# A fused attention, Fourier mixing and FFN kernel: batch 2's updates, group 1's preparation, the last W2 sums and the last stores are moved

## The chip, the cores and the metric

The kernel runs on one core of one Trainium2 chip. The time is the device time of one execution in microseconds (us). The kernel before was timed in three runs (median 777.29 us), and one more execution was recorded by the hardware profiler.

The engines are named as in the profile: PE (TensorE matmuls), PEld (its weight loads), DVE (VectorE), ACT (ScalarE), POOL (GpSimd), SP (the engine that issues DMAs here). A name with a q behind it (SPq) is that engine's queue. Each engine works through its own instructions in a fixed order.

## The reference

```
x = sink_window_attention(q, k, v)     # 4 batches, 8 heads, 768 tokens, 64 per head; 4 sink tokens, window 128
X = real(fft(fft(x, axis=tokens), axis=512 features))
u = x + X
un = (u - mean(u)) / sqrt(var(u) + 1e-6)          # over the 512 features
out = u + max(un @ w_ch1, 0) @ w_ch2              # w_ch1: 512 x 2048, w_ch2: 2048 x 512
```

All of it is float32. A matmul in full precision is made here from a high and a low part of each operand ("hi" and "lo", type fp32r): hi*hi + hi*lo + lo*hi. So most tensors are followed by a cast on ACT (hi) and a subtraction on DVE or POOL (lo).

## The kernel before

**Attention and Fourier transform.** The attention runs as a software pipeline of 96 steps (4 per block of 128 tokens, 24 blocks), with the steps that follow for what is still in the pipe. Into each step events are hung: `at(s, engine, fn)` makes `fn` be issued in step s on one engine's turn. The turns of a step come in the order S (loads), A (ACT), four numbered ones, V (DVE), G (POOL), T (PE). When the fourth block of a batch is stored, `fourier` hangs that batch's events behind that step: step 73 for batch 2 (the third batch), step 97 for batch 3 (the last). They are:
- folds of the first half of the tokens onto the second (`fold_n`, L347, then `fold_m`, L354 and L357) for j = 0, 1, 2, beginning at offsets 0, 4 and 8, with the hi cast on ACT (`fold_hi`, L360, tile gh) and the lo part on DVE (`fold_lo`, L363, tile gl). For the last batch all folds are on DVE (`FOLD_TAIL` = "VV")
- the middle row: `mid_sum` (L367) and `mid_row` (L371 the hi copy into sph, L373 its lo part), both on DVE
- stage 1 on PE (za, zr, zb, L390), casts of these to SBUF (L397, L405), stage 2 on PE (dc and a, L417; b, L438), copies of dc and a on ACT (`dc_copy`, L421, into the one-buffered tile dcs; `a_copy`, L426)
- `combine` (L443, L444): a - b and a + b into a tile d of three buffers
- `update` (L452 to L455): d is added to two blocks of u, one with the features in order and one reversed, two instructions each. For batches 2 and 3 the first is on DVE and the second on POOL (`UPD_TAIL` = "VG"). Batches 0 and 2 stay in SBUF; those of 1 and 3 are stored to DRAM.

An update of batch 2 is hung at offset `max(UPD_LATE + n, k) + 1`, n = 0 to 5, where k is the offset at which its combine is reached; with UPD_LATE = 24 k is always the larger.

**The order.** Up to step 97 (`CUT`) the order on each engine is that of the program. From there to the end of the first FFN group the order is made by the language's planner, which takes the program's order as a priority and its own modelled times for the rest. The FFN of groups 1 to 5 is again in the program's order.

**Weights.** The weights arrive as 64-bit values and are brought into shape by `convert(i)`, i = 0 to 31 (2f for w_ch1's slice f, 2f + 1 for w_ch2's): three instructions on DVE (L596 to L598), a hi cast on ACT (L620), the lo part on POOL (L621). For the first two w_ch2 slices the converted value itself is not kept; after the attention POOL adds hi and lo again into w2r (L1110), from which the W2 sums are made later.

**FFN, group 0.** The 24 blocks of tokens make six groups of four. Group 0 runs over 16 slices f of the hidden layer: `ch1` (12 matmuls of 512 columns, L632), relu on ACT and its lo part on DVE (L1121, L1126), `ch2` of the slice before (12 matmuls, L1133). In each f two steps of the remaining events are issued (`PER_F` = 2), so that steps 110, 111 fall on f = 0, and so on, and two weights are converted. At f = `PREP` = 11 the tiles of the relu are exchanged for others (h_sums; the tile un_last also begins here), and `prepare(1)` begins: statistics and normalisation of group 1's four blocks (L510 to L534), four turns on PE (L540), and hi (L544) and lo (L549) of the turned blocks into un_last. It is a generator of 20 pieces, and four are taken in each f from PREP on.

**FFN, groups 1 to 5.** Here w_ch2's product is made by a scheme of Strassen's kind: pairs q = 0 to 7 of hidden slices, seven products per pair (`product`, L1307), each of two halves (tp) of three matmuls of 256 columns. Its left operands are sums of the hidden layer (`first_h`, `second_h`, `third_h`: L1255 to L1268, tile h_sums). Its right operands, sums of W2, are made once, during group 1, stored to DRAM (w2s), and read again for each pair of the later groups in five loads by SP (`load_w2`, L1288) into one set of tiles WC (shown as w_ring and w2t). As there is one set, a load can only be issued when the products of the pair before have read the tile. The products of a pair run interleaved with `ch1` of the next pair.

**The end.** After the last pair `finish_last` makes its seven products and adds the seven accumulators p1 to p7 into the four quarters of the output, x11, x12, x21, x22 (each 128 partitions by two blocks by 256 features; L1329 is the helper `add`, L1382 the copy of p1 to s1, L1391 the sum s2 = s1 + p7). Four stores on SP, one per block of 128 x 512, follow when all quarters of two blocks are complete (L1399). Behind that, each engine reads a flag and branches (L1485, L1486) over a general version of the kernel that these inputs don't need.

Of the kernel before, what the change touches and what calls it, by code (L numbers as in the profile page):

```python
# [11 lines left out]
F32 = mybir.dt.float32  # L12
# [7 lines left out]
P = 128  # L20
# [24 lines left out]
Q_KEYS = (0, 1, 2, 4, 5, 6)  # L45
PTB = 3
W_FOLD = 6
NWA, PER_F, PREP = 14, 2, 11
FOLD_TAIL, UPD_TAIL = "VV", "VG"
UPD_LATE = 24  # L50
DSB, LDB = 3, 3
CONV_AT, CH1_AT = (3, 5, 7, 9), (9, 10)
CUT, MAN0 = 97, False
# [157 lines left out]
def kernel(  # L211
# [54 lines left out]
    def run(general):  # L266
        tag = "g" if general else ""
        with ExitStack() as p1:
# [59 lines left out]
            def fourier(b, at, ready):  # L328
# [36 lines left out]
                def mid_sum():  # L365
                    r = t_["x0"]
                    V.tensor_tensor(r[:, 1:256], r[:, 1:256], r[:, 511:256:-1], op=ALU.add)  # L367

                def mid_row():
                    t = t_["x0"]  # L370
                    V.tensor_copy(sph[:NR, :257], t[:, :257])  # L371
                    lo = sph[NR - 1:NR, :257]
                    V.tensor_tensor(lo, t[NR - 1:NR, :257], f32(lo), op=ALU.subtract)  # L373

# [95 lines left out]
                    at(k + F_S[1], "V", lambda j=j: fold_lo(j))  # L470
                at(ready[0] + ROW[0], "V", put_row)
                at(ready[0] + ROW[1], "V", mid_sum)
                at(ready[0] + ROW[2], "V", mid_row)
                k = ready[2] + S1
                n1, na, nb = PARTS_TAIL if tail else PARTS[b]
# [110 lines left out]
            def convert(i, pool=None):  # L586
# [14 lines left out]
                if i < 4:  # L601

                    if i == 0:
                        state["ring"] = npool.tile([P, 8, 512], F32R, tag="ring", name="w_ring", bufs=1)
                    d = [state["ring"][:, 2 * i + j] for j in range(2)]
                    if which:
                        state["w2t", f] = state["ring"][:, 2 * i:2 * i + 2]
                elif which:

                    if f == 2:  # L610
                        state["w2t", f] = pool.tile([P, 2, 512], F32R, name="w2t2")
                    d = [state["w2t", f % 3][:, j] for j in range(2)]
                elif W_FOLD <= f < W_FOLD + NHALF:

                    if f == W_FOLD:
                        state["fold"] = [npool.tile([P, NHALF, DM], F32R, tag=t, name=f"w_{t}", bufs=1) for t in ("gh", "gl")]
                    d = [t[:, f - W_FOLD] for t in state["fold"]]
                else:
                    d = [pool.tile([P, 512], F32R, name=f"w{i}_{j}") for j in range(2)]
                A.copy(d[0], tf)  # L620
                G.tensor_tensor(d[1], tf, f32(d[0]), op=ALU.subtract)  # L621
                Wt[f, which] = d
# [484 lines left out]
            ps_o = p1.enter_context(tc.tile_pool(name="ps_o" + tag, bufs=1, space=PSUM, side="right"))  # L1107
            wa = p1.enter_context(tc.tile_pool(name="wa" + tag, bufs=1, side="right"))
            for f in range(2):
                G.tensor_tensor(w2_raw(f, wa).bitcast(F32), *(f32(x) for x in Wt[f, 1]), op=ALU.add)  # L1110
            pg = ExitStack()
            g0 = pg.enter_context(tc.tile_pool(name="g0" + tag, bufs=1, side="right"))
            def relu(g, f, ps):
# [168 lines left out]
                V.tensor_tensor(t2, b22, t1, op=ALU.subtract)  # L1282
                V.tensor_tensor(t4, b21, t2, op=ALU.subtract)

            def load_w2(q, i):

                c, k, n, at_ = PARTS_W[i]
                nc.sync.dma_start(f32(WC[c][:, :, 2 * P * k:2 * P * (k + n)]), w_dram[q][:, :, 2 * P * at_:2 * P * (at_ + n)])  # L1288
# [9 lines left out]
                V.tensor_tensor(lo, src, f32(hi), op=ALU.subtract)  # L1298
                nc.sync.dma_start(w_dram[q][:, :, 2 * P * at_:2 * P * (at_ + n)], f32(t))

            def product(acc, q, i, tp):

                a, (c, k) = i, RIGHT[i]
                hi, lo = (t[:, 2 * P * a + P * tp:2 * P * a + P * tp + P] for t in (hc_hi, hc_lo))
# [69 lines left out]
            def finish_last(g, acc, q):  # L1374

                (x11, x12), (x21, x22) = halves(g)
                p1, p7, p2, p4, p5, p6, p3 = (bank2(t) for t in acc)
                s1, s2 = wl.tile([P, 2, 2 * P], F32, tag="u2", name=f"u2_{g}", bufs=1), r4[:, 0]
                for i in range(4):
                    for tp in range(2):  # L1380
                        product(acc, q, i, tp)
                A.copy(s1, p1)  # L1382
                add(G, x11, s1)
                add(V, x21, p4)
                add(V, x11, p2)
                for i in (5, 4, 6):
                    for tp in range(2):
                        product(acc, q, i, tp)
                add(V, s1, p6)
                add(G, x12, s1)  # L1390
                V.tensor_tensor(s2, s1, p7, op=ALU.add)  # L1391
                add(G, x21, s2)
                add(V, x22, p5)
                add(V, x22, s2)
                add(V, x12, p5)
                add(V, x12, p3)
                for t in (1, 0):
                    for b, blk in groups[g][2 * t:2 * t + 2]:
                        nc.sync.dma_start(out[b, blk], u_of(b, blk))  # L1399

            prev, late, turns = None, iter(()), []
            with tc.manual_schedule():
                w_sums(0)
# [2 lines left out]
                for g in range(1, len(groups)):  # L1406
                    unT = state[g][1]
                    steps = iter(())
                    for q in range(NF // 2):
# [12 lines left out]
                        if prev is not None:  # L1422
# [4 lines left out]
                                finish_a(*prev[:2])  # L1427
                            if g == 1:
                                w_sums(q)
                            else:  # L1430
                                load_w2(q, 1)
                                load_w2(q, 0)
                        if q == 1 and g == 1:
                            finish(0, po, us, slice(1, 4))
                        elif q == 1:
                            finish_c(*old)
                            late = finish_d(old[0])
# [6 lines left out]
                        slot(prev, slice(7, 14))  # L1444
                        second_h()
                        if g > 1:
                            for i in range(2, 5):
                                load_w2(q, i)
                        elif q:
                            for i in (1, 0, 2):  # L1450
                                split_w(q, i)
# [113 lines left out]
```

## Time and profile before

| | |
|---|---|
| runs | 777.29 us (median of 3; 776.57 to 779.79) |
| the profiled execution | 777.47 us, span of its instructions 775.7 us |
| PE busy | 741.1 us (96% of the span) |
| DVE busy | 601.3 us (78%) |
| ACT busy | 344.1 us (44%) |
| POOL busy | 186.4 us (24%) |
| mean granted clock of PE | 0.993 |

The attention and the Fourier transform fill the span until about 240 us, group 0 of the FFN ends about 337 us, and groups 1 to 5 take the rest. In a row of the timeline stand start, length (us), engine, line, operation, output and inputs, shapes and count; in brackets the engine's idle time ahead of it and what ended that. In the chain of waits each row is a piece of work (start, length, engine, tile, line), and the pieces together lead to the last instruction. In the windows the columns behind the length are busy us (and instructions) of PE, PEld, DVE, ACT and POOL, the granted clock, the busy share of the DMA engines and GB/s.

### The profile page before, as it was taken

To read this page: it belongs to the slowest core of one execution; us is meant where nothing else is said; L and a number is where in the kernel's file an instruction comes from. 1 tells how busy PE (TensorE), PEld (TensorE's weight loads), DVE (VectorE), ACT (ScalarE), POOL (GpSimd) and SP (SyncE) were. 2 spreads that over 40 slices of the span, in tenths; PEclk is the share of its full clock that TensorE was granted. 3 is DMA by queue.
4 is the path that set the end of the run, shared out by engine and by line. 5 is a ranking of instruction groups with operands and counts; after the bars stand their busy time and mean duration, and the time that the engine had idled before them with its cause. 6 is when DMAs were issued, how large, how long until landed. Compare 5 with 4: busy or idle time off the path is not lost.

```text
span 775.7 us, 14193 instructions
## 1 busy us (share of the span) xinstructions
PE 741.1 (96%) x4915; PEld 626.8 (81%) x4915; DVE 601.3 (78%) x1640; ACT 344.1 (44%) x893; POOL 186.4 (24%) x288
## 2 busy tenths in 40 slices
PE   7999998998989999999999999999999999999993
PEld 5666776766777878778888989989999989998992
DVE  6778589789799989959877978778895788664344
ACT  5777666666633323344545333333343334432330
POOL 2557368377555445300000000000000000000002
PEclk9999999999999999999999999999999999999997
DMA  9845515533304456224446766655666557555653
GB/s 292 266 125 155 142 55 166 142 110 113 110 28 122 151 190 217 92 100 165 161 168 227 231 188 214 229 184 170 210 213 216 171 177 232 165 188 176 220 175 113
DMA packets 96224, 131.23 MB, mean 169 GB/s; under 512 B 5996, under 2 KB 61420, under 8 KB 95760
## 3 DMA queue, kind: packets, MB, share of 16 engines
q1 hardware_dynamic: 95856, 126.49, 51.2%
q0 software_dynamic: 288, 3.76, 1.2%
q8 instruction: 41, 0.67, 0.4%
q14 instruction: 39, 0.32, 0.1%
HBM read 106.09 MB, written 24.13 MB: 168 GB/s over the span
## 4 chain that ended last, share of the span: by engine, by line
PE 80%; DVE 13%; ACT 2%; issue 2%; DMA 1%; POOL 1%; SPq 0%; ACTq 0%; DVEq 0%; POOLq 0%
PE h L632 32%; PE p L1307 25%; PE o L1133 4%; PE xt L802 4%; PE s L715 4%; PE za L390 2%; PE pt L764 2%; PE zb L390 1%; DVE f L347 1%; DVE sm L733 1%; PE zr L390 1%; DVE s L721 1%; PE x L814 1%; DVE gl L363 1%; DMA vt<-in_v_sink_dram 1%
## 5 line engine op out<-in xcount | busy, mean ns | idle before, releaser
L1307 PE MATMUL p<-w_ring,h_sums 128*128 128x256 f32 x960 | 134.5, 283 | 1.9 <-DMA w_ring<-w2s 1.7
L1307 PEld LDWEIGHTS p<-w_ring,h_sums 128*128 128x128 f32 x960 | 126.0, 191 | 5.4 <-issue 1.9
L1255 ACT CAST h_sums<-sums 128x256 fp32r<-128x256 f32 (+2 forms) x160 | 90.8, 567 | 70.9 <-PE p L1307 31.3
L1307 PE MATMUL p<-w2t,h_sums 128*128 128x256 f32 x720 | 112.9, 283 | 0.0
L1256 DVE TENSOR_TENSOR h_sums<-sums,h_sums 128x256 fp32r<-128x256 f32 (+2 forms) x160 | 99.5, 622 | 15.1 <-ACT h_sums L1255 14.0
L1329 POOL TENSOR_TENSOR u<-u,u 128x512 f32<-128x512 f32 x2 | 2.8, 1376 | 434.9 <-ACT u L1382 431.3
L1307 PEld LDWEIGHTS p<-w2t,h_sums 128*128 128x128 f32 x720 | 100.3, 191 | 3.1
L632 PE MATMUL h<-un_last,w 128*128 128x512 f32 x396 | 96.5, 392 | 0.0
L632 PE MATMUL h<-un_slots,w 128*128 128x512 f32 x396 | 96.3, 391 | 0.0
L632 PEld LDWEIGHTS h<-un_slots,w 128*128 128x128 f32 x396 | 72.7, 188 | 14.1
L632 PEld LDWEIGHTS h<-un_last,w 128*128 128x128 f32 x396 | 72.2, 188 | 14.5 <-DVE un_slots L549 0.7
L739 ACT ACTIVATE sm<-sm,mx 128x132 f32<-128x132 f32 x192 | 75.9, 400 | 14.4 <-DVE mx L733 14.4
L1441 ACT ACTIVATE sums<-h 128x512 f32<-128x512 f32 x40 | 23.9, 598 | 98.3 <-PE h L632 98.3
L715 PE MATMUL s<-ring,q 64*128 64x260 f32 x320 | 55.1, 426 | 8.0 <-DVE mx L733 7.8
L1157 DVE STREAM_TRANSPOSE unf<-un 32x128 f32<-32x128 f32 x192 | 58.1, 302 | 2.8
L1266 DVE TENSOR_TENSOR sums<-sums 128x256 f32<-128x256 f32 x40 | 16.9, 421 | 49.2 <-ACT sums L1441 48.9
L1411 ACT ACTIVATE sums<-h 128x512 f32<-128x512 f32 x40 | 24.0, 599 | 66.8 <-PE h L632 66.8
L733 DVE CUSTOM_DVE_ANT_0 sm<-s,mask 128x132 f32<-128x132 f32 x192 | 47.5, 284 | 3.9 <-PE s L713 2.0
L721 DVE COPY_PREDICATED s<-older,s 128x256 f32<-128x256 uint8 x80 | 33.8, 422 | 14.9 <-PE s L715 14.7
L715 PEld LDWEIGHTS s<-ring,q 64*128 64x128 f32 x320 | 24.8, 184 | 22.1 <-issue 10.3
L802 PE MATMUL xt<-ptl,ldv 128*64 128x128 f32 x384 | 39.0, 285 | 0.0
L739 ACT ACTIVATION_READ_ACCUMULATOR sm<-sm,mx 128x1 f32 x192 | 36.7, 191 | 0.0
(236 smaller groups left out, 1369.3 us busy)
## 6 DMA issues: line engine op xcount, KB each, us to landing
w_ring<-w2s SPq DMA_DIRECT2D x64, 512.0 KB, 4.3
w2t<-w2s SPq DMA_DIRECT2D x96, 256.0 KB, 3.2
raw<-in_moe_w_ch_dram SPq DMA_DIRECT2D x32, 512.0 KB, 3.4
w2s<-w_ring SPq DMA_DIRECT2D x16, 512.0 KB, 3.0
ldv<-in_v_dram SPq DMA_DIRECT2D x28, 256.0 KB, 2.8
ring<-in_qk_dram SPq DMA_DIRECT2D x24, 264.0 KB, 4.8
w2s<-w2t SPq DMA_DIRECT2D x24, 256.0 KB, 3.0
out_dram<-u SPq DMA_DIRECT2D x24, 256.0 KB, 4.3
```

The costliest lines, as they stand in the source:

```text
L390: T.matmul(ps[:, :NK], a, c, start=i == 0, stop=i == len(mm) - 1)
L632: T.matmul(ps[:, :tb], a[:, cs], x[:, :, cc, :], start=n == 0, stop=n == 3 * NCC - 1)
L715: T.matmul(ps[:, j, :P + W], st["q", g][rows, hp, :], keys(g, 2 * hp + j), start=True, stop=True)
L721: V.copy_predicated(ps[:, :, P + NS:P + W], older[qi > 2], ps[:, :, 0:P])
L733: V.tensor_tensor_reduce(sm[:, h % 4], ps[:, j, P:P + W], mask[min(qi, 3)], -SCALE, 3.0e38, ALU.add, ALU.min, accum_out=mx[:, 0, h:h + 1])
L739: A.activation(sm[:, h % 4], sm[:, h % 4], AF.Exp, bias=mx[:, 0, h:h + 1], scale=-1.0, accum_out=mx[:, 1, h:h + 1])
L802: T.matmul(ps[D * j:D * j + D, p, :], st["v", kb(g) - i][:, h, :], a[:, h % 4, :], start=i == 0, stop=i == n - 1)
L1133: T.matmul(po[i], a[:, ts_], x, start=f == 0 and n == 0, stop=f == NF - 1 and n == 2)
L1157: V.transpose(unf[32 * q:32 * q + 32, :, r], un[r].rearrange("p (c q j) -> p c q j", c=NCC, q=4)[:, :, q])
L1255: A.copy(hc_hi[:, left(a, n)], src)
L1256: V.tensor_tensor(hc_lo[:, left(a, n)], src, f32(hc_hi[:, left(a, n)]), op=ALU.subtract)
L1307: T.matmul(acc[i][:, 2 * P * tp:2 * P * tp + 2 * P], x, w, start=q == 0 and tp == 0 and n == 0, stop=q == NF // 2 - 1 and n == 2, skip_gro ...
```

## The change

- `UPD_LATE` goes from 24 to 40, so that batch 2's updates are hung at steps 114 to 119.
- `PREP` goes from 11 to 10.
- The hi copy of the middle row becomes an event of its own (`mid_hi`); for the last batch it is on ACT, ahead of `mid_row`.
- For the first two w_ch2 slices the converted value is kept in its tile, and ACT copies it into w2r in place of POOL's sum.
- The W2 sums of the last pair of the last group are loaded in that group's first pairs (q = 1 to 5, one load each) into tiles of their own, WL, which lie in un_slots (the buffer of the even groups' normalised blocks). The last pair's five loads into WC fall away.
- `finish_last` makes its products in the order 0, 1, 5, 2, 3, 4, 6, adds in another order, gives x22 + s2 to POOL, and stores the four quarters instead of the four blocks: x11 and x12 by ACT's queue, x21 and x22 by SP's.

```diff
-NWA, PER_F, PREP = 14, 2, 11
+NWA, PER_F, PREP = 14, 2, 10
 FOLD_TAIL, UPD_TAIL = "VV", "VG"
-UPD_LATE = 24
+UPD_LATE = 40
...
+                def mid_hi():
+                    (A.copy if b == B - 1 else V.tensor_copy)(sph[:NR, :257], t_["x0"][:, :257])
+
                 def mid_row():
                     t = t_["x0"]
-                    V.tensor_copy(sph[:NR, :257], t[:, :257])
                     lo = sph[NR - 1:NR, :257]
...
+                at(ready[0] + ROW[2], "A" if b == B - 1 else "V", mid_hi)
                 at(ready[0] + ROW[2], "V", mid_row)
...
+                if which and f < 2:
+                    state["cv", f] = t
                 A.copy(d[0], tf)
...
             for f in range(2):
-                G.tensor_tensor(w2_raw(f, wa).bitcast(F32), *(f32(x) for x in Wt[f, 1]), op=ALU.add)
+                A.copy(w2_raw(f, wa).bitcast(F32), state.pop(("cv", f)).bitcast(F32))
...
-                for i in range(4):
+                for i in (0, 1, 5, 2, 3, 4, 6):
                     for tp in range(2):
-                        product(acc, q, i, tp)
+                        product(acc, q, i, tp, WL)
                 A.copy(s1, p1)
                 add(G, x11, s1)
-                add(V, x21, p4)
-                add(V, x11, p2)
-                for i in (5, 4, 6):
-                    for tp in range(2):
-                        product(acc, q, i, tp)
                 add(V, s1, p6)
                 add(G, x12, s1)
                 V.tensor_tensor(s2, s1, p7, op=ALU.add)
+                add(V, x11, p2)
+                add(V, x21, p4)
                 add(G, x21, s2)
                 add(V, x22, p5)
-                add(V, x22, s2)
+                add(G, x22, s2)
                 add(V, x12, p5)
                 add(V, x12, p3)
-                for t in (1, 0):
-                    for b, blk in groups[g][2 * t:2 * t + 2]:
-                        nc.sync.dma_start(out[b, blk], u_of(b, blk))
-
+                for t, d, x, e in ((0, 0, x11, A), (1, 0, x21, nc.sync), (0, 1, x12, A), (1, 1, x22, nc.sync)):
+                    b, blk = groups[g][2 * t]
+                    e.dma_start(out[b, blk:blk + 2].rearrange("n p w -> p n w")[:, :, 2 * P * d:2 * P * d + 2 * P], x)
+
+            LAST = len(groups) - 1, NF // 2 - 1
+            assert LAST[0] % 2
+            wl_ = un_slots.rearrange("p a b c t -> p (a b c t)")
+            WL = [wl_[:, 1024 * c:1024 * c + (1024 if c < 3 else 512)].rearrange("p (j w) -> p j w", j=2) for c in range(4)]
...
-                            else:
+                            elif (g, q) != LAST:
                                 load_w2(q, 1)
                                 load_w2(q, 0)
+                            if g == LAST[0] and 0 < q <= len(PARTS_W):
+                                load_w2(LAST[1], q - 1, WL)
...
-                            for i in range(2, 5):
+                            for i in range(2, 5) if (g, q) != LAST else ():
                                 load_w2(q, i)
```

`load_w2` and `product` take the set of tiles (WC or WL) as an argument.

More of the change, by code (lines that the diff above doesn't have):

```diff
@@ L1283, in w_sums, with load_w2 @@
                 V.tensor_tensor(t4, b21, t2, op=ALU.subtract)
-            def load_w2(q, i):
+            def load_w2(q, i, WC=WC):
                 c, k, n, at_ = PARTS_W[i]
@@ L1299, in split_w, with product @@
                 nc.sync.dma_start(w_dram[q][:, :, 2 * P * at_:2 * P * (at_ + n)], f32(t))
-            def product(acc, q, i, tp):
+            def product(acc, q, i, tp, WC=WC):
                 a, (c, k) = i, RIGHT[i]
```

## The prediction

> **What bounds the kernel now.** I read the page's first line, then the windows by stage, then TensorE's timeline for its waits, then the chain that ended last. The page, then four of the windows:
>
> ```profile
> span 775.7 us, 14193 instructions
> ```
>
> ```profile
> 200.00:240.00 40.00, 35.88 (x248) 29.48 (x247) 37.15 (x79) 17.04 (x47) 23.37 (x27) 0.96 0.18 56
> 240.00:280.00 40.00, 40.00 (x203) 34.38 (x202) 37.74 (x69) 11.42 (x23) 19.92 (x17) 1.00 0.45 150
> 280.00:320.00 40.00, 39.41 (x176) 32.15 (x175) 36.48 (x55) 13.32 (x24) 20.74 (x16) 1.00 0.62 204
> ...
> 760.00:776.00 16.00, 2.38 (x18) 2.21 (x18) 6.22 (x8) 0.00 (x0) 2.50 (x2) 0.74 0.22 80
> ```
>
> The columns behind the length are busy us of PE, PEld, DVE, ACT and POOL. From 240 to 760 PE hardly stops: nothing there is to be won except where it stops. It stops in three places that the change touches: just before 240, around 330, and after 760. DVE is 93% busy in the first of them and 94% in the stage behind it, so DVE is the rival bound of the whole middle. In the timeline PE's waits stand in brackets, with what ended them:
>
> ```profile
> 234.20 0.62 PE L390 MATMUL za<-cst,gh 128*128 128x386 f32 x2 [3.13 <-ACT gh L360]
> 235.24 0.98 PE L390 MATMUL za<-cst,gh 128*128 128x386 f32 x2 [0.42 <-DVE d L444]
> ...
> 281.55 0.50 PE L632 MATMUL h<-un_slots,w_gl 128*128 128x512 f32 x1 [0.59 <-POOL w_gl L621]
> ...
> 328.70 0.63 PE L540 MATMUL unt<-ident,un 128*128 128x128 f32 x4 [0.84 <-DVE un_last L549]
> ...
> 334.10 0.51 PE L632 MATMUL h<-un_last,w_ring 128*128 128x512 f32 x1 [0.90 <-ACT un_last L544]
> 334.83 2.79 PE L632 MATMUL h<-un_last,w_ring 128*128 128x512 f32 x11 [0.22 <-DVE un_last L549]
> ```
>
> **Part 1, the updates behind the folds.** PE's 3.13 us wait is for the last fold of batch 3 (gh, cast by ACT after fold_m at L354). The chain that ended last runs through DVE there:
>
> ```profile
> 221.72 1.03 DVE u L454
> 222.75 0.87 DVE u L455
> ...
> 226.60 0.78 DVE u L454
> 227.38 1.43 DVE u L455
> 228.80 0.74 DVE sph L371
> ...
> 233.08 0.41 DVE f L354
> ```
>
> Four update instructions of batch 2 and the sph copy stand in front of L354. Batch 2's events count from step 73 and batch 3's from 97. UPD_LATE 40 moves the updates to steps 114 to 119 (73 + 41 to 73 + 46), past the last fold's end at 97 + 8 + 5 = 110; the sph copy goes to ACT, which is busy 17.04 of 40. They sum to 1.03 + 0.87 + 0.78 + 1.43 + 0.74 = 4.85, so L354 comes up to 4.85 earlier. The combine that ends the 0.42 wait is behind it on DVE and comes with it. PE's 3.13 + 0.42 = 3.55 go, and 1.3 us of DVE's lead are left over.
>
> What is next late: DVE must still do the updates. At L354's price for this width (0.41) two instructions of three updates cost 2.5 us; at the crowded price of the chain (4.11 for four) 6.2. DVE's idle in 200 to 280 is 2.85 + 2.26 = 5.1, and among its work there are group 1's statistics, needed only for the turns (L540) tens of us later. POOL's half moves too (the groups by line, 215 to 300):
>
> ```profile
> L455 POOL TENSOR_TENSOR u<-u,d 128x255 f32<-128x255 f32 x3 | 4.1, 1366 | 0.0
> ...
> L454 POOL TENSOR_TENSOR u<-u,d 128x257 f32<-128x257 f32 x3 | 3.1, 1043 | 6.1 <-DVE d L452 6.1
> ...
> L1110 POOL TENSOR_TENSOR w2r<-w_ring 128x512 f32<-128x512 f32 x2 | 2.8, 1412 | 1.6 <-issue 1.6
> ```
>
> These 7.2 us go among the weight conversions on POOL's queue (L621), and who waits for those is ch1. The first that they can delay are those of f = 3 and later (timeline):
>
> ```profile
> 244.33 1.84 POOL L621 TENSOR_TENSOR w<-cv,w 128x512 fp32r<-128x512 f32 x1 [1.29 <-ACT w L620]
> ...
> 250.50 2.89 PE L632 MATMUL h<-un_slots,w 128*128 128x512 f32 x12
> ```
>
> It ends at 246.17 and is used at 250.50: 4.3 us of cover, 0.8 once PE is 3.55 earlier. The two sums of L1110 (2.8 us) leave POOL for two copies on ACT, idle 23 of 40 there: nothing on the path, and POOL's queue is shorter by it. So PE's gain lies between 0 (DVE or POOL take it all back) and 3.55 + 0.59 = 4.1 (the wait at 281.55 closes as well). I take 3.0, near the upper rows, since cover exists for most of what is moved.
>
> No DMA is moved by this part: batch 2 is resident, so its updates store nothing.
>
> **Part 2, preparation a step sooner.** The three waits for un_last are 0.84 + 0.90 + 0.22 = 1.96. One step of the group-0 loop:
>
> ```profile
> 297.47 2.88 PE L632 MATMUL h<-un_slots,w 128*128 128x512 f32 x12
> ...
> 302.91 2.88 PE L632 MATMUL h<-un_slots,w 128*128 128x512 f32 x12
> ```
>
> is 5.44 us, so the last piece of un_last comes up to 5.4 earlier and all three waits close. Price: four un_make and four un_lo, 128x512 each, come a step earlier on DVE. At up to 0.69 (the row of that size in part 3) they are 5.5 us over three steps; DVE's idle in 280 to 320 is 3.52 of 40, 1.4 in three steps; 4.1 would be uncovered. The conversions on DVE run ahead of PE by
>
> ```profile
> 315.54 1.29 POOL L621 TENSOR_TENSOR w<-cv,w 128x512 fp32r<-128x512 f32 x1 [1.38 <-ACT w L620]
> ...
> 319.59 3.02 PE L632 MATMUL h<-un_slots,w 128*128 128x512 f32 x12
> ```
>
> 319.59 - 316.83 = 2.8 us. Also the relu that must wait for ch2 before its tile exists moves from f = 11 to f = 10; PE had no wait behind it at 11. Bounds: 1.96 gained, and 4.1 - 2.8 = 1.3 lost. Before, one of those three steps (f = 13) stood beside conversions already, with no wait of PE on them; so I take 1.7, near the upper end.
>
> **Part 3, the end.** The timeline, with the products (L1307), the sums (L1329) and the stores (L1399):
>
> ```profile
> 756.83 0.88 PE L1307 MATMUL p<-w_ring,h_sums 128*128 128x256 f32 x6
> ...
> 757.77 0.96 DVE L1256 TENSOR_TENSOR h_sums<-sums,h_sums 128x768 fp32r<-128x768 f32 x1 [0.61 <-ACT h_sums L1255]
> ...
> 758.41 1.47 POOL L1329 TENSOR_TENSOR u<-u,u 128x512 f32<-128x512 f32 x1 [431.34 <-ACT u L1382]
> ...
> 761.61 1.67 PE L1307 MATMUL p<-w_ring,h_sums 128*128 128x256 f32 x12 [1.74 <-DMA w_ring<-w2s]
> ...
> 763.39 0.69 DVE L1391 TENSOR_TENSOR sums<-u,p 128x512 f32<-128x512 f32 x1
> ...
> 764.67 1.26 POOL L1329 TENSOR_TENSOR u<-u,sums 128x512 f32<-128x512 f32 x1
> 764.71 1.77 DVE L1329 TENSOR_TENSOR u<-u,sums 128x512 f32<-128x512 f32 x1
> ...
> 766.55 3.65 SPq L1399 DMA_DIRECT2D out_dram<-u  x4
> ```
>
> The early W2 sums remove the 1.74. Their five loads go to SP in q = 1 to 5 of the last group, behind loads that themselves wait for PE; SP's queue has the room. Its waits between 660 and 745:
>
> ```profile
> SPq L1288 <- PE p L1307: 59.0, 25, 3.6
> ```
>
> 59 of those 85 us SP waits for PE, and an issue takes 0.43 (the row of L1399 below): I cost the five at nothing. If that cover were gone, PE would wait some 0.43 a pair, 2.2 in all. Products now come in the order 0, 1, 5, 2, 3, 4, 6, some 0.75 us each (12 take 1.67, 6 take 0.88). Product 5 is third, at 758.3, and its lo matmul needs the 768-wide split, done at 758.73: about 0.3 of stall. PE ends near 756.83 + 7 x 0.75 + 0.3 = 762.4.
>
> DVE's first add (s1 and p6) waits for POOL's first (758.41 + 1.47 = 759.9). Seven DVE instructions at 0.67 follow, all with a PSUM operand, which POOL does not slow (0.69 at 763.39): x11 is done by the third at 761.9, x21 has p4 by the fourth at 762.6, x12 is done by the seventh at 764.6. POOL: x12 until 762, then x21 (needs that fourth) 762.7 to 764.0, then x22 until 765.3. Stores: x11 and x12 on ACT at 762.0 and 764.7, x21 and x22 on SP at 764.0 and 765.3. The collision of 764.71 (1.77 us beside POOL) is gone, and SP issues two stores instead of four. The stores' own rows (us from issue to landing in the last), and SP's last wait:
>
> ```profile
> L1399 SPq DMA_DIRECT2D out_dram<-u x4: 338/428/1833, 766.5 to 769.8; - x4
> ...
> DMA to landing us min/median/max: 2.9/4.2/4.3
> ```
>
> ```profile
> SPq L1486 <- SPq L1486: 2.6, 1, 2.6
> ```
>
> Before, SP's last issue ends at 766.55 + 3.65 = 770.2 and the span 5.5 later; 2.6 of that is SP's branch at L1486, which this change leaves. The last landing (769.8 + 2.9 = 772.7) is earlier than the code needs. After: last issue 765.3 + 0.43 = 765.75, end 771.25, a gain of 4.45. Bounds below it: one issue of 1.83 among the two (end 772.65), or a landing of 4.3 that now sets the end (769.6, and 3.0 behind it as 775.7 - 772.7: 772.6). So 3.05 to 4.45; ACT issues no DMA in this trace, and I price its issue by SP's. I take 4.0.
>
> [...]
>
> [...]
>
> **Sum.** 3.0 + 1.7 + 4.0 = 8.7. The profiled execution took 777.47 (span 775.7 and 1.8 around it), so 768.8; the median of the three runs is 0.18 lower, so 768.6.
>
> **Rivals.**
> 1. DVE takes the front gain back: PE is early, but the conversions, updates and statistics on DVE and POOL set the pace until 281. Then part 1 gives only what DVE itself loses, 0.74 (the sph copy). For it: 94% busy DVE. Against it: the statistics in that stretch can wait. Time 777.29 - 0.74 - 1.7 - 4.0 = 770.9.
> 2. The change does less than it says. From step 97 on a planner, not the text, orders each engine, by its own modelled times, and it may put the updates back between the folds, as it hoists group 1's statistics; the un_last chain may also stay late. Then only the end pays: 774.2 with its 3.05, 772.8 with its 4.45.
> 3. Slower. dcs has one buffer, and batch 2's last update reads it at step 119, the very step at which batch 3's dc row is to be copied into the next one:
>
> ```profile
> 236.29 0.41 DVE L452 COPY d<-dcs 1x514 f32<-1x514 f32 x1
> ...
> 263.25 0.35 ACT L421 COPY dcs<-dc 1x257 f32<-1x257 f32 x1
> ```
>
> If that update comes late, ACT holds the PSUM bank of dc and with it every later Fourier product on PE. With PE 3.55 early the copy is due at 259.7; each us of the update's end beyond that costs PE one. It decides from 259.7 + 3.0 + 5.7 = 268.4 on; ending at 274 it would cost 14.3 against those 8.7, and the time is 777.29 + 5.6 = 782.9. Against it: before, the update's first piece (L452) ran at 236.29, and its inputs come no later now, so it has 23 us of room.
>
> **How the numbers follow.** A measurement can tell about 0.5% (3.9 us) from no change, so faster means under 773.4. The forecast has 0.50, rival 1 0.22, rival 2 0.19, rival 3 0.06, and 0.03 is left for what I do not see. Forecast and rival 1 are faster throughout (0.72). Rival 2's span, 772.8 to 774.2, lies across the line: 0.08 faster, 0.11 same. Rival 3 is slower with 0.04 and within 0.5% with 0.02; the 0.03 count as same. So faster 0.80, same 0.16, slower 0.04. The lower end takes every upper bound (4.1 + 1.96 + 4.45 = 10.5, 766.8) and 0.8 for DVE instructions no longer crowded by L1110: 766.0. The upper end is the tail alone at its least, 774.2.
>
> **What would show it.** Right: no wait on gh of over 0.5 us near 230; none on un_last near 325; no DMA wait on w_ring at the end; the span's end some 15 us behind the first product of the end (18.9 before: 775.7 - 756.83); x22 the last store on SP; L1486's 2.6 still there. Wrong: new waits of PE on L621 or L1126 between 235 and 285 as long as those removed (rival 1), L454 still among the L347 (rival 2), ACT's L421 late (rival 3), or a last landing that ends behind SP's code.

## The result, and the profile after

The changed kernel took 770.53 us (median of six runs, 769.82 to 772.01), the kernel before beside it 777.38 (six runs, 775.38 to 779.79): a ratio of 0.991 (95% interval 0.9895 to 0.9934). In a second measurement, on one chip with the partial kernels below, it took 768.42 against 777.42: 0.988 (0.985 to 0.9904). The forecast of 768.6 lies between the two medians.

The profiled execution of after took 772.01 us. Its page's first line, and its windows at the places shown of before (busy us of PE, PEld, DVE, ACT and POOL, granted clock, DMA share, GB/s):

```profile
span 770.1 us, 14184 instructions
```

```profile
200.00:240.00 40.00, 39.20 (x284) 32.02 (x281) 37.13 (x82) 21.09 (x59) 21.53 (x24) 1.00 0.22 73
240.00:280.00 40.00, 38.23 (x193) 32.64 (x192) 38.77 (x71) 10.28 (x21) 17.31 (x16) 1.00 0.40 138
280.00:320.00 40.00, 39.42 (x175) 32.13 (x174) 36.74 (x56) 14.27 (x24) 20.05 (x16) 1.00 0.62 204
```

The first row is the gain: PE idles 0.80 us where it idled 4.12 (this execution runs 2.70 us later there, which the stages below take out). The second is a price: PE idles 1.77 us in a stretch where it was busy for all 40.00 before, and DVE's idle there falls from 2.26 to 1.23. PE's waits in the timeline of after (L392 was L390, L637 was L632, L1138 was L1133, L543 was L540):

```profile
232.85 0.62 PE L392 MATMUL za<-cst,gh 128*128 128x386 f32 x2
...
235.27 0.60 PE L392 MATMUL za<-cst,gh 128*128 128x386 f32 x2 [0.51 <-DVE d L446]
...
261.01 1.00 PE L419 MATMUL a<-cst,za 128*128 128x258 f32 x6 [1.37 <-DVE zb L407]
...
270.05 2.57 PE L1138 MATMUL o<-w_ring,h 128*128 128x512 f32 x10 [0.39 <-DVE h L1131]
...
281.91 0.50 PE L637 MATMUL h<-un_slots,w_gl 128*128 128x512 f32 x1 [0.58 <-POOL w_gl L626]
...
323.31 0.63 PE L543 MATMUL unt<-ident,un 128*128 128x128 f32 x4 [0.35 <-DVE un_last L552]
...
327.86 0.63 PE L543 MATMUL unt<-ident,un 128*128 128x128 f32 x4 [0.28 <-DVE un L537]
```

The 3.13 us wait on gh is gone, and the second pair of stage-1 matmuls takes 0.60 instead of 0.98 us: before, it ran at half clock behind the wait. New are the two waits on DVE at 261 and 270. Of the 1.96 us on un_last 0.35 is left, with 0.28 on un. The end of after (products L1312, adds L1334, stores L1401):

```profile
755.46 5.57 PE L1312 MATMUL p<-un_slots,h_sums 128*128 128x256 f32 x42
...
758.54 0.69 DVE L1334 TENSOR_TENSOR u<-u,p 128x512 f32<-128x512 f32 x1 [1.18 <-POOL u L1334]
...
760.58 2.96 ACTq L1401 DMA_DIRECT2D out_dram<-u  x2
761.23 2.49 POOL L1334 TENSOR_TENSOR u<-u,sums 128x512 f32<-128x512 f32 x2 [0.61 <-DVE u L1334]
762.52 1.61 SPq L1401 DMA_DIRECT2D out_dram<-u  x2
```

The 42 matmuls of the seven products run in one piece, without the wait on w_ring, for 5.57 us: the prediction's own 7 x 0.75 + 0.3. x22 is done on POOL at 763.72, 8.26 us behind the first product (predicted 765.3 - 756.83 = 8.5), and SP's last issue ends at 764.13. The last quarter lands 4.4 us behind its issue of 763.74, some 1.9 us before the span's end, so the code behind the stores still sets the end. SP's branch behind it is still there (the waits of SP; total, times, longest):

```profile
SPq L1494 <- SPq L1494: 3.2, 2, 2.9
```

**Where the time went.** The span is cut at starts of PE's matmuls: the last attention scores; the first ch1 of f = 9; the first ch1 of group 1; the first product of the FFN; the first product of the end; the span's end. In us:

| | before | after | after, second time | gain (before - after) |
|---|---|---|---|---|
| start to last scores | 206.34 | 209.04 | 206.21 | -2.70 |
| to ch1 of f = 9 (front) | 85.69 | 83.33 | 83.33 | 2.36 |
| to group 1, and on to the first product | 42.07 + 11.51 | 40.98 + 10.88 | 40.99 + 10.88 | 1.72 |
| to the end's first product | 411.22 | 411.23 | 411.12 | -0.01 |
| end | 18.92 | 14.64 | 14.39 | 4.28 |

The three parts gained 8.36 us, and 2.70 went where the change touches nothing that had begun. That loss is the clock. In the windows at the attention the column behind POOL's is the granted clock; first after, then after the second time:

```profile
120.00:125.00 5.00, 2.58 (x24) 1.61 (x23) 4.96 (x15) 2.25 (x9) 4.92 (x7) 1.00 0.46 126
125.00:130.00 5.00, 5.00 (x33) 2.90 (x31) 3.17 (x19) 3.57 (x12) 4.28 (x9) 0.54 0.59 173
130.00:135.00 5.00, 5.00 (x34) 4.05 (x31) 2.34 (x9) 2.14 (x9) 0.00 (x0) 0.78 0.87 302
```

```profile
125.00:130.00 5.00, 4.81 (x51) 3.52 (x48) 4.02 (x20) 3.67 (x13) 4.29 (x9) 1.00 0.62 201
130.00:135.00 5.00, 5.00 (x40) 3.63 (x40) 4.59 (x20) 3.40 (x15) 2.54 (x6) 1.00 0.72 275
```

In the first execution the clock was halved from 125.40 for 6.83 us; in the second not at all. The same kernel has both.

### The profile page after: what moved, and what is told of

It is laid out like the page before. It is cut to its first block, busy times and chain, and to the rows that moved or that the text cites. A ratio compares the mean times of both kernels' runs of the same rounds, so it can differ in the third digit from the quotient of the medians.

```text
span 770.1 us, 14184 instructions
## 1 busy us (share of the span) xinstructions
PE 742.7 (96%) x4915; PEld 627.2 (81%) x4915; DVE 597.2 (78%) x1638; ACT 346.1 (45%) x896; POOL 183.1 (24%) x287
## 4 chain that ended last, share of the span: by engine, by line
PE 78%; DVE 15%; issue 2%; ACT 2%; POOL 1%; DMA 1%; SPq 0%; DVEq 0%; ACTq 0%; POOLq 0%
PE h L637 30%; PE p L1312 25%; PE xt L807 5%; PE s L720 5%; PE o L1138 3%; PE pt L769 2%; PE za L392 2%; PE zb L392 1%; DVE f L347 1%; PE x L819 1%; DVE sm L738 1%; DVE gl L363 1%; PE zr L392 1%; DVE w2r L601 1%; DMA vt<-in_v_sink_dram 1%
## 5 line engine op out<-in xcount | busy, mean ns | idle before, releaser
L1312 PE MATMUL p<-w_ring,h_sums 128*128 128x256 f32 x936 | 131.1, 283 | 0.1
L1312 PEld LDWEIGHTS p<-w_ring,h_sums 128*128 128x128 f32 x936 | 122.9, 191 | 3.5 <-DVE u L1142 0.3
L1312 PE MATMUL p<-w2t,h_sums 128*128 128x256 f32 x702 | 110.2, 283 | 0.0
L1334 POOL TENSOR_TENSOR u<-u,u 128x512 f32<-128x512 f32 x2 | 2.8, 1384 | 429.0 <-ACT u L1387 428.2
L1312 PEld LDWEIGHTS p<-w2t,h_sums 128*128 128x128 f32 x702 | 97.9, 191 | 3.1
L637 PE MATMUL h<-un_last,w 128*128 128x512 f32 x396 | 96.5, 392 | 0.0
L637 PE MATMUL h<-un_slots,w 128*128 128x512 f32 x396 | 96.5, 392 | 0.0
L637 PEld LDWEIGHTS h<-un_last,w 128*128 128x128 f32 x396 | 72.3, 188 | 14.5 <-DVE un_slots L552 0.7
L637 PEld LDWEIGHTS h<-un_slots,w 128*128 128x128 f32 x396 | 72.7, 188 | 14.0
L776 ACT COPY pta<-pt 128x512 f32<-128x512 f32 x48 | 28.1, 585 | 21.1 <-PE pt L769 20.5
```

The costliest lines, as they stand in the source:

```text
L637: T.matmul(ps[:, :tb], a[:, cs], x[:, :, cc, :], start=n == 0, stop=n == 3 * NCC - 1)
L776: A.copy(a, st.pop(("pt", g, hp // 2)))
L1312: T.matmul(acc[i][:, 2 * P * tp:2 * P * tp + 2 * P], x, w, start=q == 0 and tp == 0 and n == 0, stop=q == NF // 2 - 1 and n == 2, skip_gro ...
```

## The experiments

The theory: the three parts are independent, each is worth about its term, and what the first measurement lacks is the half clock in the attention. The rivals: the parts share a gain, or DVE takes the front's back.

**The kernel after again, and its parts alone.** after_again is the changed kernel as it stands. tail_only is it with the edits of the front and of PREP undone, prep_only is the kernel before with one number changed, front_only the kernel before with these lines:

```diff
-UPD_LATE = 24
+UPD_LATE = 40
...
+                at(ready[0] + ROW[2], "A" if b == B - 1 else "V", mid_hi)
...
-                G.tensor_tensor(w2_raw(f, wa).bitcast(F32), *(f32(x) for x in Wt[f, 1]), op=ALU.add)
+                A.copy(w2_raw(f, wa).bitcast(F32), state.pop(("cv", f)).bitcast(F32))
```

> The changed kernel once more, unaltered, for a second profile. In its first profile TensorE's granted clock was at half from 125.4 to 132.2 us, in a stretch where the two kernels' orders are the same, and the last attention scores came 2.7 us later than before. Theory 'chance': that half-clock stretch is not the change's doing, so it will be missing in some executions of this kernel; where it is missing the span is 768.5 and the front is 2.7 us earlier at the last scores. Rival 'caused': something in the change brings it about, and it is there every time at the same place. Median expected by both: 770.5, ratio 0.991.

> The kernel before with part 3 alone (early W2 sums of the last pair, regrouped sums and stores). The stretch from the first product of the end to the end of the span was 18.9 us before and 14.6 after. Theory 'parts add': this alone is worth those 4.2, 773.1. Rival 'shared': some of the 4.2 comes from PE reaching the end in another state because of parts 1 and 2, and the part alone is worth 3 or less, 774.4 or more.

> The kernel before with part 1 alone (updates behind the folds, sph copy and w2r copies on ACT). Counted from the last attention scores, the first product of the end came 4.1 earlier after the change, of which 2.4 stood already ahead of ch1 of f = 9. Theory 'parts add': 2.4 of gain, 775.0. Rival 'taken back': without the preparation a step sooner the waits for un_last grow by what PE comes earlier, and nothing is left, 777.4.

> The kernel before with PREP = 10 alone. Theory 'parts add': the gain between ch1 of f = 15 and the first product of group 1, less what DVE loses in f = 13 to 15, is 1.7: 775.7. Rival 'needs part 1': with the updates in their old place DVE is no freer, the conversions become late by what the preparation takes, and the gain is under 0.7, 776.7 or more.

Measured, against a kernel before of 777.42 us: after_again 768.42 (0.988, interval above), tail_only 774.34 (0.996, 0.9936 to 0.9979), front_only 774.75 (0.997, 0.9946 to 0.9984), prep_only 776.36 (0.999, 0.9965 to 1.0005). The stages of the profiled executions are sharper than these medians: to f = 9 83.33 in front_only and 85.67 to 85.72 in the other two; to the first product 51.87 in prep_only (40.99 + 10.88) and 53.50 to 53.59 in the others; the end 14.06 in tail_only, 17.60 and 17.33 in the others. Each part alone moves its own stage by what it is worth in the whole, and leaves the others, but for the old end's own spread (below). In the stages the gains add up. The medians alone don't show it: they gain 3.08, 2.67 and 1.06, together 6.81, where after_again gains 9.00; tail_only's 774.34 lies at its rival's bound (774.4), prep_only's 776.36 between its theory and its rival, with an interval that includes no change. The median granted clocks differ too (0.991 in tail_only, 0.993 in front_only, 0.988 in prep_only, 0.996 in after_again), so the rest is most likely the clock; that is argued, not shown.

**The updates without the rest of the front.** updates_only is the kernel before with `UPD_LATE = 40`; updates_sums has the W2 sums as ACT copies too, and leaves the sph copy on DVE.

> The kernel before with UPD_LATE = 40 and nothing else: the sph copy stays on DVE, the two W2 sums stay on POOL, preparation and end are the old ones. The stretch is taken from the last attention scores to the first ch1 matmul of f = 9 (85.7 us before, 83.33 with the whole front). If the four updates ahead of L354 were nearly all of the front gain: 83.5 to 83.9, the wait on gh down to about 0.8 us and no half clock behind it. If the sph copy (0.74 us ahead of the last fold) and the W2 sums on POOL carried a third of it: 84.3 to 84.6. If the updates alone are given back on DVE and POOL (the first rival of the prediction): 85.3 to 85.7.

> The kernel before with UPD_LATE = 40 and the two W2 sums as ACT copies, but with the sph copy still on DVE. With UPD_LATE alone the last fold (L354) came 24.85 us after the last scores, against 26.74 before and 21.91 with the whole front, since the fold instructions themselves had grown longer. Theory: POOL's two W2 sums (some 3 us) run beside the folds and stretch them; moved to ACT, the last fold is at 22.4 to 23.2 (0.74 for the sph copy above the whole front's) and the stretch to f = 9 is 83.3 to 84.3. Rival: the sph copy, or the order that ACT gets, is what holds the fold: 24 or more, and the stretch 85.0 to 85.9.

To f = 9: 85.89 us in updates_only and 82.94 in updates_sums, against 85.69 before and 83.33 in front_only. The last fold (L354) comes 26.74 us behind the last scores before, 24.84 in updates_only, 22.22 in updates_sums and 21.91 in front_only. Four updates of 4.11 us are gone from ahead of it in updates_only, yet it gains only 1.9. updates_only's 85.89 lies just above all three of its ranges; updates_sums beats its theory, with both figures just below the ranges. DVE and POOL there, from the timeline of updates_only:

```profile
227.59 1.40 DVE L373 TENSOR_TENSOR sph<-xr,sph 1x257 fp32r<-1x257 f32 x1
229.00 2.17 DVE L347 TENSOR_TENSOR f<-us,us 128x512 f32<-128x512 f32 x2
```

```profile
225.46 3.25 POOL L1110 TENSOR_TENSOR w2r<-w_ring 128x512 f32<-128x512 f32 x2 [0.24 <-POOL u L454]
228.67 0.91 POOL L455 TENSOR_TENSOR u<-u,d 128x255 f32<-128x255 f32 x1
229.54 1.08 POOL L454 TENSOR_TENSOR u<-u,d 128x257 f32<-128x257 f32 x1
```

and of updates_sums:

```profile
228.40 0.75 DVE L373 TENSOR_TENSOR sph<-xr,sph 1x257 fp32r<-1x257 f32 x1
229.16 1.29 DVE L347 TENSOR_TENSOR f<-us,us 128x512 f32<-128x512 f32 x2
```

```profile
226.88 0.74 POOL L455 TENSOR_TENSOR u<-u,d 128x255 f32<-128x255 f32 x1
227.57 1.30 POOL L454 TENSOR_TENSOR u<-u,d 128x257 f32<-128x257 f32 x1
```

The same DVE instructions take 1.40 and 2.17 us where POOL works beside them, and 0.75 and 1.29 where it works less or not. With the updates out of the way, DVE's next instructions move up to where POOL does its sums and, behind them, its own updates of batch 2, and take over the slowness that DVE's updates had. Between the two timelines of before and updates_only, one L347 grows from 1.12 to 1.37, one L357 from 0.41 to 0.95, L373 from 0.75 to 1.40 and the last two L347 from 1.29 to 2.17: 2.32 together, which is what is missing (4.11 - 1.90 = 2.21) to 0.1. Why they are longer there was not shown.

In updates_only PE still waits 3.24 us, and the last thing that ends it is another one:

```profile
233.90 1.01 PE L390 MATMUL za<-cst,gh 128*128 128x386 f32 x2 [3.24 <-ACT asb L426]
```

```profile
232.47 0.62 ACT L360 CAST gh<-f 128x512 fp32r<-128x512 f32 x1 [5.42 <-DVE f L354]
233.00 0.59 ACT L1121 ACTIVATE h<-h 128x512 fp32r<-128x512 f32 x1
233.49 0.37 ACT L426 COPY asb<-a 128x257 f32<-128x257 f32 x1
```

gh is there at 233.09; ACT then does a relu and the copy of a, which frees PSUM. Some of the 85.89 is the clock: its half-clock stretch at 232.6 lasted 6.83 us, not the 3.41 of before, and before_filled (below), with the same 6.83, needs 86.41 where before needs 85.69. So the updates alone are worth some 0.5 at the most (86.41 - 85.89, one execution each), and with the W2 sums off POOL 2.75. The W2 sums' move without the updates' was not run: how the gain splits between the two holds for this order of adding them. The sph copy's move is no gain: the whole front is 0.39 slower to f = 9 than updates_sums, though its fold is 0.31 earlier; the six profiles with the whole front lie between 83.29 and 83.34. Why was not followed, nor was the whole change run with that copy left on DVE.

**What DVE takes back.** Between f = 2 and f = 9 the changed kernel loses again some of what it had gained at f = 2 (30.96 us behind the last scores, 35.33 before, a gain of 4.37). no_dve_updates and no_updates leave out batch 2's updates, on DVE or on both engines:

```diff
+                    if b == B - 2 and not rev:
+                        return
                     x = 1 if rev else 0
```

In no_updates the condition is `b == B - 2` alone.

> The changed kernel in which batch 2's three DVE updates (the blocks with the features in order, six instructions, some 5 us of DVE) are left out; those blocks of u lack their mixing term, and everything else is as in the changed kernel. Theory: the front is 83.33 us from the last scores to f = 9 because DVE, which still does the moved updates, is late for PE at f = 4 to 6, where some 2 us of the gain at f = 2 are lost again. Then the stretch is 81.0 to 82.0 here, and the short waits of PE on DVE and POOL between 261 and 282 us shrink by as much. Rival: POOL's conversions and the Fourier order on PE itself set that pace: 83.0 to 83.4, nothing gained.

> The changed kernel in which all six updates of batch 2 are left out, those on DVE and those on POOL (twelve instructions and a copy); batch 2's blocks of u lack their mixing term. Without the three on DVE the stretch from the last scores to f = 9 was 82.24 us, against 83.33 with them; from f = 2 to f = 9 it was 51.27 against 52.37, and 50.37 before the change. Theory: POOL's updates, which stand among its weight conversions, cost the other 0.9 of what is lost behind f = 2: the stretch is 81.2 to 81.7. Rival: that 0.9 is lost to something else (the conversions and group 1's statistics, which now come closer together): 82.0 to 82.4.

To f = 9: 82.24 us, between the theory's range and the rival's, and 81.38, inside its theory's range, though not for the theory's reason. From f = 2 to f = 9: 50.36 before, 52.37 after, 51.27 without the DVE updates, 51.06 without any. So of the 2.01 lost, 1.10 is DVE's updates and 0.21 POOL's. (POOL's cost 0.64 more ahead of f = 2, 30.32 against 30.96. Two of its three updates of batch 2 did not move behind the folds at all.) POOL's timeline of after shows them beside DVE's folds of 222 to 231 us, and only the third behind:

```profile
225.13 0.91 POOL L457 TENSOR_TENSOR u<-u,d 128x255 f32<-128x255 f32 x1
226.00 0.89 POOL L456 TENSOR_TENSOR u<-u,d 128x257 f32<-128x257 f32 x1
226.85 0.73 POOL L457 TENSOR_TENSOR u<-u,d 128x255 f32<-128x255 f32 x1
227.54 0.82 POOL L456 TENSOR_TENSOR u<-u,d 128x257 f32<-128x257 f32 x1
...
248.48 0.64 POOL L456 TENSOR_TENSOR u<-u,d 128x257 f32<-128x257 f32 x1 [3.84 <-DVE d L454]
```

The other 0.70 needs no update at all. In the timelines of no_dve_updates and no_updates, the wait on zb:

```profile
260.77 0.99 PE L419 MATMUL a<-cst,za 128*128 128x258 f32 x6 [0.98 <-DVE zb L407]
```

```profile
258.60 0.99 PE L419 MATMUL a<-cst,za 128*128 128x258 f32 x6 [0.77 <-DVE zb L407]
```

1.37 with all updates, 0.77 with none, nothing before. In no_updates DVE is busy 31.32 us between 240 and 280, against 38.77 in after, so this rest is not its load: PE has caught up with the lo part of zb on DVE (L407). Which instruction ahead of that one could go was not tried.

**The end, piece by piece.** old_stores is the changed kernel with the four block stores on SP; late_w2 is it with the five late loads of the last pair in place of the early ones (the conditions around the loads are put back too).

```diff
-                        product(acc, q, i, tp, WL)
+                        product(acc, q, i, tp)
...
```

> The changed kernel with the four stores of whole blocks back on SP behind all the sums; early W2 sums and the new order of products and adds stay. From the first product of the end to the span's end: 14.4 to 14.8 us with the quarters on two queues, 17.3 to 18.9 before. Theory: the stores' regrouping is worth 1.3 to 2.7 us, as all four issues then stand behind POOL's last sum (8.3 us behind that product) and one of them is a long one: 15.7 to 17.4. Rival: the end hangs on SP's code behind the stores or on the last landing, and the regrouping is worth nothing: 14.4 to 15.0.

> The changed kernel with the last pair's W2 sums loaded late again, by the five old loads into the old tiles; products, adds and stores of the end are the new ones. Theory: the wait of PE on the DMA comes back in the middle of the products, which then take 6.4 to 7.2 us instead of 5.57, and the end is 15.3 to 16.4 instead of 14.4 to 14.8. Rival: the new order of products leaves the load enough time, or the wait only takes the place of the stall for the 768-wide split: 5.5 to 5.9, and the end is unchanged.

The ends are 16.08 us, inside the theory's range, and 18.26, above both ranges; the changed end in its six profiles (after, after_again, tail_only, no_dve_updates, no_updates, after_filled) is 14.06 to 14.77. The regrouped stores are worth some 1.7. In old_stores, POOL's last adds, and SP's four issues behind them:

```profile
758.48 2.49 POOL L1334 TENSOR_TENSOR u<-u,sums 128x512 f32<-128x512 f32 x2 [0.62 <-DVE u L1334]
760.99 2.14 SPq L1401 DMA_DIRECT2D out_dram<-u  x4
```

The early W2 sums are worth more than the 1.74 of their old wait, some 3.8 (18.26 - 14.41, the mean of the six), which neither the theory nor the rival had. late_w2:

```profile
751.61 1.60 PE L1312 MATMUL p<-w_ring,h_sums 128*128 128x256 f32 x12
...
758.65 2.90 PE L1312 MATMUL p<-w_ring,h_sums 128*128 128x256 f32 x12 [3.28 <-DMA w_ring<-w2s]
761.35 1.16 PE L1312 MATMUL p<-w2t,h_sums 128*128 128x256 f32 x6
762.35 0.88 PE L1312 MATMUL p<-w_ring,h_sums 128*128 128x256 f32 x6
```

In the new order the late load is needed after two products, not four, so the wait is 3.28; behind it PE runs at half clock for 3.41 us (12 matmuls take 2.90 instead of 1.60). So the new order needs the early loads: without them the end is about as long as before. The early loads under the old order were not run.

**The half clock in the attention.** PE has an idle of 2.4 us there, in every kernel; in after_again, where no half clock followed:

```profile
123.97 0.71 PE L720 MATMUL s<-ring,q 64*128 64x260 f32 x4 [2.40 <-DVE mx L738]
```

before_filled and after_filled put 16 transposes of no use into it:

```diff
+                        at(61, "T", lambda: warm_up(16, ps_t.tile([P, 4, P], F32, tag="pt", name="keep")))
```

> The kernel before with 16 more transposes of 128x128 on PE in step 61, their result unused, in the 2.4 us idle of PE at 121.5 us of the attention. Theory: the half clock of 3.41 or 6.83 us at 124 to 132 us, which appears in some executions of either kernel, comes from that idle; filled, no execution has it: the median falls to 775 to 776.5 us and the slowest ones go. The half clock at 235 us, behind the 3.13 us wait on gh, stays. Rival: that half clock has another cause: it shows in some executions as before, and the median is the kernel before's 777.4, or some 0.5 more for the added work.

> The changed kernel with the same 16 transposes in the 2.4 us idle of PE at 121.5 us. Theory: without the half clock in the attention its median is 767.5 to 768.5 us with a spread of under 1.5 us, some 8 us below the kernel before with the same filling, which is the sum of the three stage gains (2.4 + 1.7 + 4.2). Rival: the half clock has another cause: it appears in some executions as before, the median is 768.4 to 770.5 and the spread over 2 us.

Measured: before_filled 776.39 us (775.08 to 778.63, 12 runs; ratio 0.998, 0.9963 to 0.9997), after_filled 768.77 (768.27 to 770.17, six runs; 0.989, 0.9865 to 0.9911), the kernel before 777.37 (775.66 to 782.2, 17 runs). From after_filled:

```profile
120.64 1.97 PE L886 MATMUL keep<-ident 128*128 128x128 f32 x16
123.05 0.71 PE L720 MATMUL s<-ring,q 64*128 64x260 f32 x4 [0.43 <-DVE mx L738]
```

```profile
125.00:130.00 5.00, 4.71 (x43) 3.55 (x41) 4.03 (x17) 3.80 (x14) 3.54 (x7) 1.00 0.82 261
130.00:135.00 5.00, 5.00 (x41) 3.63 (x39) 4.22 (x19) 2.83 (x12) 3.28 (x8) 1.00 0.61 229
```

Neither profiled execution with the filling has the half clock. Of the twelve without, four have none (last scores at 205.57 to 206.34), four have 3.41 us of it (207.18 to 207.88) and four 6.83 (208.80 to 209.18), on the mean 1.4 and 2.9 us later. If it struck two executions in three anyway, two free ones would come up one time in nine; by the count alone the filling as its cure is likely, not shown.

The clock records of the profiles say more. Between the clock's changes lie whole multiples of 3.41 us (in before 228.69 us at full clock, 67 of them), on a grid whose place differs between executions. Counted in windows of this grid, the eight executions with the half clock have 1.88 to 2.42 us of PE's idle in the window ahead of it. In the four without it the grid splits the 2.4 us, and no window near 122 has more than 1.65 (before), 1.35 (after_again), 1.53 (prep_only) and 1.24 (old_stores). In all fourteen profiles, of 3088 windows at full clock, the 27 with 1.88 us or more of idle are each followed by half clock, and the 3061 with 1.85 or less by full clock (idle by the profile's modelled ends of matmuls). In before and after alone, the four followed by half clock have 1.98, 2.68, 2.79 and 3.41 us, and none of the other 438 has over 1.65. One such window of before, and one of after, behind which the clock is halved:

```profile
122.42:125.84 3.42, 1.77 (x21) 1.29 (x22) 3.39 (x15) 1.49 (x7) 3.27 (x7) 1.00 0.03 8
```

```profile
121.98:125.40 3.42, 1.44 (x18) 1.13 (x20) 3.38 (x14) 1.16 (x5) 3.27 (x7) 1.00 0.08 23
```

By these counts the idle is most likely the cause, and where the grid happens to lie the chance; how the clock is set was not shown. In the filled kernels no window of the attention has over 1.03 us of idle. Why the half clock lasts one window in some executions and two in others was not found.

before_filled's median lies inside its theory's range, and none of its twelve runs has a mean clock under 0.989, where three of the seventeen beside it have (0.984 to 0.987). after_filled's median falls outside what the theory gave (767.5 to 768.5), its spread of 1.90 is between the two theories, and it does not beat after_again: as a step for the kernel it is worth nothing that was measured. The two filled kernels differ by 776.39 - 768.77 = 7.6 us.

## Why the prediction was right

Its likeliest case came about: all three parts pay, the sum was 8.7, and the stages of the profiled pair gained 8.36. The first median is 1.9 above the forecast, most likely because the half clock in the attention struck its runs more, which is chance: their mean granted clocks were 0.991 to 0.994, those of the second measurement 0.995 to 0.997. A stretch of 3.41 us at half clock lowers that mean by 1.7 / 770 = 0.0022. That it also explains each run that was not profiled is argued, not shown.

- **Part 1, the size.** Taken at 3.0, got 2.36. "4.85 earlier" holds for the last fold, 26.74 - 21.91 = 4.83, but partly by luck: it needs the move of the W2 sums, which the sum had at nothing (next point). "PE's 3.13 + 0.42 = 3.55 go" was 3.13 - 0.09: the wait behind the combine is 0.51 now. What f = 2 gained beyond that, 4.37 - 3.04 = 1.33, is most likely the half clock behind the wait (3.41 us of it before, none in after), which had not been priced; before_filled, with 3.41 us more of it, reaches f = 2 1.09 later than before. Against it stand the 2.01 lost between f = 2 and f = 9. That is rival 1's mechanism, with part of its price.
- **Part 1, the reason.** The step that failed is "nothing on the path" for the two W2 sums of L1110, and with it the 4.11 at the crowded price as the updates' own. The updates alone bring the fold 1.90 forward and f = 9 at most 0.5; the W2 sums' move brings the fold another 2.62 and f = 9 the rest. The sph copy's 0.74, counted as a gain, was 0.31 for the fold and -0.39 at f = 9.
- **Part 1, the rest.** POOL's cover for L621 held: the wait at 281.55 is there as before (0.59, now 0.58). "The wait at 281.55 closes" was the upper bound, and did not. Batch 2's three DVE updates, bounded by 2.5 and 6.2, took 3.2 + 2.3 = 5.5. "POOL's half moves too" came true for one update of three.
- **Part 2.** Taken at 1.7, got 1.72. The waits give 1.96 - 0.35 - 0.28 = 1.33 of it; where the other 0.4 comes from was not followed. The same edit alone gains 1.71 in this stage (prep_only, 53.58 - 51.87).
- **Part 3.** Taken at 4.0, got 4.28. The product order, DVE's and POOL's instants and the 2.6 of SP's branch (2.9 now) came out within 0.3 us. But the end of before is no fixed length: in the six profiles with the old end it is 17.03 to 18.92, mean 17.81, and the profiled one was the longest. Against the new mean of 14.41 the part is worth 3.4, so that 4.0 was met is partly luck; tail_only's median gains 3.08. What the 1.83 us issue was no run shows; the longest of the four issues was 0.74 to 1.83 in those six, and the longest issue 0.43 in every end with two queues. The landings there took up to 4.5 us (no_dve_updates), near the 4.3 of the rows.
- **Rivals.** Rival 2 fell for DVE: the planner put no update back between its folds (DVE's first L456 of batch 2 is at 236.39, behind L354). For POOL it held in part: two of POOL's three updates stayed at 225 to 228 us (above), and without any updates the last fold comes 21.23 us behind the last scores, against 21.92 with POOL's alone. Rival 3 fell with room: the copy out of dcs (now L454) ran at 247.99, the dc copy at 263.13.

```profile
236.39 1.50 DVE L456 TENSOR_TENSOR u<-u,d 128x257 f32<-128x257 f32 x1
...
247.99 0.41 DVE L454 COPY d<-dcs 1x514 f32<-1x514 f32 x1
```

## What to carry to other kernels

An instruction's length beside a busy neighbour was not its own here (L373 took 1.40 us beside POOL's sums, 0.75 without them): before it is counted as the gain of moving it, look at what will stand in its place and whether the neighbour is still there. Here, added behind the updates' move, the move of POOL's sums brought the larger half of a gain that the prediction had put down to DVE's updates. Cut both spans at the same instructions and compare stage by stage; a stage that the change doesn't touch then shows what belongs to the clock, and an edit that another one needs (the loads, for the order of products) shows as a part that costs more to undo than it seemed to win.

## What the runs showed of the hardware

- A single idle of 2.4 us on PE was followed, in eight of twelve executions, by 3.41 or 6.83 us at half clock, and the waits of 3.13 us (before), 3.24 (updates_only) and 3.28 (late_w2) by half clock too. Counted in windows of 3.41 us on the grid of the clock's own changes, the 27 with 1.88 us of idle or more were each followed by half clock, the 3061 with 1.85 or less never (fourteen profiles).
- So two waits of some 3 us cost more than themselves: before, the wait on gh took 3.13 us and its half clock most likely some 1.3 more; in late_w2 the 3.28 us on the DMA were followed by 1.30 more on twelve matmuls (2.90 - 1.60).
- Some of DVE's instructions with two inputs, both in SBUF, took up to 3.6 times as long with POOL at work beside them: 1.40 in updates_only against 0.75 in updates_sums (L373), 2.17 against 1.29 (two L347), and 1.50 at 236.39 in after, beside POOL's L626 of 235.88 to 237.62, against 0.42 for the same update at 235.02 in before, where POOL was idle. Not all did: L363 at 226.88 in updates_only, beside L1110, kept its 0.68.
